# Third chunk of a retention recurrence in halves of 64 tokens, and one visit of the fourth chunk behind another inner product

## The chip, the cores and the metric

The kernel runs on one core of a Trainium2 chip. The metric is the device time of one execution in microseconds (us); the median of several executions is compared. Engines are named as in the profile: PE (TensorE matmul), PEld (its weight loads), DVE (VectorE), ACT (ScalarE), POOL (GpSimd), SP (SyncE, whose queue issues nearly all the DMAs).

## What is computed

A retention recurrence over 768 tokens (4 batches, 8 heads of 64 dimensions), whose output, with the heads side by side, goes through a feed-forward block of 512 by 2048 with a leaky ReLU:

```python
for t in range(S):
    state = gamma[None, :, None, None] * state + np.einsum('bhd,bhe->bhde', k[:, :, t], v[:, :, t])
    y[:, :, t] = scale * np.einsum('bhd,bhde->bhe', q[:, :, t], state)
x = y.transpose(0, 2, 1, 3).reshape(B * S, H * D)
h = x @ w_in
out = np.maximum(0.01 * h, h) @ w_out
```

Everything is in 32-bit floats.

## The kernel before

The tokens are worked in six chunks (c = 0 to 5) of 128 tokens per batch, 512 tokens in all. The feed-forward block of a chunk is worked in four units (u = 0 to 3) of 512 of the 2048 hidden columns. Both of its products use Strassen's seven products, named M1 to M7, each a group of eight matmul records on the full array.

Chunks 0 and 1 run first and together (`hidden` and `output`, recorded at L628). Each is a generator of seven steps; `run` calls, after each step, whatever the tables `hidden_more` and `output_more` (L1053 to L1075) list under s0 to s6 for (chunk, unit). In this phase the weights are unpacked too: `next_mantissas` on DVE (L556 to L568), whose ends let SP load the next pieces; the sums of the weights (`sum_of_unit`, L972) are formed, and `keep_unit` (L1001) stores each unit to DRAM.

Chunks 2 to 5 run in the loop at L1234, n = 0 to 15, four units for each chunk. The hidden product is there `inner(n, group)` (L1140) for two groups of output columns. It is written by hand: M1, M5, M4, M6, M2, M3, M7 into banks 0 to 3 of PSUM. ACT copies M1 from bank 0 to bank 3 (L1153), M6 is added to it there by PE, and the other results are copied out by ACT or added by DVE. `outer(n, 1)` (L1174) makes the four blocks of g from them: five sums on DVE and four leaky ReLUs on ACT (L1184). `output` with `room` puts M1 into bank 5, M5 into bank 7 and M6 into bank 4 (`room`, L1211: A, B, C, D are banks 5, 4, 7, 6), in the order M1, M5, M6, M2, M7, M3, M4. `products(steps, n)` lets n of these seven steps be issued. The units' weights stream back from DRAM into `wa` and `wb` (`load_unit`, L1024), for the next unit as soon as a group of the present one is done, or, where `held` is set, behind the visit that follows.

The recurrence of a chunk is a visit for two batches at a time, (c, 0) and (c, 2).

For c = 1 and 2 it has the old form: `score` (L149, matmuls at L165) for each batch, `masked` on DVE (L183, recorded at L185, 128x768), and for c = 2 `visit` (L331): `reads` of the old state (L200), `last_values` (L235), `state` (L250), `first_values` (L224), then `tokens_taken` (L280) and `state_taken` (L286) on DVE. Some of these matmuls use the array as four tiles of 64x64, others as two of 128x64.

For c = 3 to 5 it has the joined form, by halves of 64 tokens. `scores_of_pair` (L348) makes the scores within each half (L360) and the two halves' sums of k times v (L371), masks the scores on DVE (L378) and adds the sums to the old state one after the other (a state in the middle of the chunk, and one at its end). `joint_visit` (L399) then makes the outputs with `read` (L414) and `value` (L431) and takes them out with four operations on DVE (L453). All these matmuls are 64x64. Afterwards it loads k and v of the next pair into the same tiles (L307), has POOL decay v (`decay_v`, L135), and loads a later pair's q and k (`ahead`). PSUM of a joint visit: banks 1 and 7 for its first batch, 0 and 2 for its second; DVE takes the second batch first, and within a batch the second bank first.

What sets the order around the change: each engine issues its instructions in the order in which the program writes them; there is no planner. For chunk 2 the tables place it: scores of (2, 2) at s0 of `hidden` (1, 3), its visit at s4, scores of (2, 0) at s6, its visit at s2 of `output` (0, 3), followed at s3 by `differ(2)` (differences of x on DVE) and `next_heads` (loads of (3, 0) and (3, 1) and their decays on POOL); the sums of x for group 0 at s6. Then, at L1215 to L1232: three products of the last output of chunk 1, `scores_of_pair(3, 0)`, two products, `inner(0, 0)`, two products, `inner(0, 1)`, `outer(0, 1)`, and `joint_visit(3, 0)`. The loop then begins with the differences of g and `inner(1, 0)`. In the loop the visits (4, 0) and (5, 0) stand behind `inner(n + 1, 0)` of u = 0, and all (c, 2) behind that of u = 1; three products after each, `scores_of_pair` of the following pair is issued.

Of the kernel before, what the change touches and what calls it, by code (L numbers as in the profile page):

```python
# [9 lines left out]
FP32 = mybir.dt.float32  # L10
# [8 lines left out]
C = 128  # L19
# [3 lines left out]
def kernel(  # L23
# [82 lines left out]
    def place_for(c, b, place=None):  # L106

        if place is None:
            x = work.tile([128, 2, HP, C], FP32, tag="qk", bufs=AHEAD, name=f"qk_{c}_{b}")
            y = work.tile([128, 2, H, D], FP32, tag="kv", bufs=AHEAD, name=f"kv_{c}_{b}")  # L110
        else:
            flat = place.rearrange("p i k n -> p (i k n)")
            half = 2 * HP * C
            x = flat[:, 0:half].rearrange("p (s a t) -> p s a t", s=2, a=HP)
            y = flat[:, half : 2 * half].rearrange("p (s h d) -> p s h d", s=2, h=H)
        heads[c, b] = x, y
# [7 lines left out]
    def load_k(c, b):  # L124
        nc.sync.dma_start(out=heads[c, b][1][:, 0], in_=kv[c, b][:, 0])

    def load(c, b, place=None):
# [202 lines left out]

    def visit(c, b):  # L331

        for f in (reads, last_values, state, first_values):
            for i in range(2):
                f(c, b + i)
        for i in range(2):
            tokens_taken(c, b + i, xs[c][0])
        for i in range(2):
            state_taken(c, b + i, for_state(sums_at[c, b + i]))
        for i in range(2):  # L340
            heads.pop((c, b + i))

    halves_of_states = []
    state_of = [states[:, 2 * p : 2 * p + 2] for p in range(B // 2)]
    mid_of = {}
    quads = [(m, i, 2 * m + i) for m in range(HP // 2) for i in range(2)]

    def scores_of_pair(c, b):  # L348

        if b == 0:  # L350
            next_gq()
        at = [bank[j].rearrange("p (b m i t) -> p b m i t", b=2, m=HP // 2, i=2)
              for j in range(2)]
        sums = [bank[2 + h].rearrange("p (b a d) -> p b a d", b=2, a=HP) for h in range(2)]
        for n in range(2):
# [28 lines left out]
        old = state_of[p]  # L384
        mid = mid_of[p] = halves_of_states.pop(0)
        plus(mid, old, sums[0])
        state_of[p] = None
        if not last:
# [9 lines left out]

    def joint_visit(c, b):  # L399

        later = following(c, b)
        at = [[bank[k].rearrange("p (a t) -> p a t", t=C) for k in banks]
              for banks in ((1, 7), (0, 2))]
        by_half = mid_of.pop(b // 2)
# [43 lines left out]
        for n in (1, 0):  # L448
            for j in (1, 0):
# [4 lines left out]
                                        in1=gq[:, j], op=ALU.mult)  # L454
        if c < NC - 1:
            halves_of_states.extend(by_half)
        for n in range(2):
            heads.pop((c, b + n))
        if later is not None:
# [4 lines left out]
            for n in range(2):  # L464
                decay_v(later[0], later[1] + n)
        for n in range(2):
            ahead(c + 1, b + n)

    def following(c, b):
# [308 lines left out]

    def scored(c, b):
        def do():  # L780
            decay_v(c, b)
            score(c, b)
            masked(c, b)
        return do

    def differ(c):
# [259 lines left out]
    def next_heads():  # L1046
# [3 lines left out]
        for b in range(2):  # L1050
# [8 lines left out]
                     s4=[lambda: load(2, 2, place_of_unit(0, "in22"))],  # L1059
                     s5=[sum_of_unit(3, 0)], s6=[sum_of_unit(3, 1)]),  # L1060
        (1, 3): dict(s0=[begin_x(2), scored(2, 2), scored(2, 3)],
                     s1=[sum_of_unit(3, 2)], s2=[sum_of_unit(3, 3)],
                     s3=[keep_unit(3)], s4=[lambda: visit(2, 2)],
                     s6=[scored(2, 0), scored(2, 1)]),
    }
# [5 lines left out]
        (1, 2): dict(s0=[sum_of_unit(2, 3)], s1=[keep_unit(2)]),  # L1071
        (0, 3): dict(s0=[begin_units], s1=[lambda: differences(*parts[1][1:])],
                     s2=[lambda: visit(2, 0)], s3=[differ(2), next_heads],
                     s6=[sums(2, 0)]),
    }  # L1075
# [196 lines left out]

JOINED = 3

# [84 lines left out]
```

## Time and profile before

| what | us |
|---|---|
| median of 9 runs (lowest, highest) | 647.38 (645.43, 648.39) |
| the profiled execution's own time | 646.12 |
| its span, first to last instruction | 644.0 |
| PE busy | 633.8 |
| PEld busy | 570.3 |
| DVE busy | 461.3 |
| ACT busy | 269.7 |
| POOL busy | 22.2 |
| granted TensorE clock | 1.000 |

How to read it: the span is cut into stages by the program's order. Up to about 225 us the first two chunks and the weights' unpacking run, and chunk 2's recurrence lies at 191 to 220 us. The rest is the loop. A matmul in the source is two records in the trace. In the timeline a line gives the start of a run of records, its length up to the end of the last one, and, in brackets, how long the engine stood idle ahead of it and what released it. Matmul records overlap, so the time that a group takes is read from its start to the start of the next group.

### The profile page before, as it was taken

How to read it: one execution, taken by the hardware profiler on the slowest of the kernel's cores; microseconds unless marked ns; L12 is line 12 of the kernel's file. 1: busy time of each engine (PE TensorE's matmuls, PEld its weight loads, DVE VectorE, ACT ScalarE, POOL GpSimd, SP SyncE). 2: the span in 40 equal slices, each digit the busy share in tenths (PEclk: the TensorE clock that was granted, in tenths of full speed). 3: DMA queues.
4: the chain of work that ended last, by engine and by line, in shares of the span. 5: the costliest groups of instructions: out<-in, count | busy, mean ns of one | idle time of the engine just before them, and what ended most of it. 6: DMA issues, size and time to landing. Idle time of an engine off the chain costs nothing.

```text
span 644.0 us, 14045 instructions
## 1 busy us (share of the span) xinstructions
PE 633.8 (98%) x5958; PEld 570.3 (89%) x5958; DVE 461.3 (72%) x756; ACT 269.7 (42%) x515; POOL 22.2 (3%) x45
## 2 busy tenths in 40 slices
PE   8999999999999998999999999999999999999997
PEld 5888888888888897998999898999989999999996
DVE  5789769889979777466785756878737778636655
ACT  5875557257253033342342342523424423534421
POOL 2000000000011010101000101000010000000000
PEclk9999999999999999999999999999999999999999
DMA  8931327455965977637544584554456336444201
GB/s 330 404 122 60 104 66 256 136 195 152 309 241 177 330 255 242 238 89 246 160 127 161 181 257 158 174 172 152 144 185 194 89 117 195 156 157 159 87 0 67
DMA packets 89263, 113.40 MB, mean 176 GB/s; under 512 B 3432, under 2 KB 71912, under 8 KB 89200
## 3 DMA queue, kind: packets, MB, share of 16 engines
q1 hardware_dynamic: 88896, 111.88, 52.6%
q8 instruction: 47, 0.77, 0.5%
q10 hardware_dynamic: 304, 0.62, 0.3%
q14 instruction: 16, 0.13, 0.1%
HBM read 93.35 MB, written 19.14 MB: 175 GB/s over the span
## 4 chain that ended last, share of the span: by engine, by line
PE 91%; DMA 4%; DVE 2%; ACT 1%; SPq 0%; issue 0%; DVEq 0%
PE bank L628 31%; PE bank L1149 27%; PE C_h L628 4%; PE B_o L628 4%; PE A_o L628 4%; PE A_h L628 4%; PE B_h L628 4%; PE C_o L628 4%; PE D_o L628 2%; PE D_h L628 2%; DMA kv<-in_kv_dram 2%; DMA x_words<-in_weights_dram 1%; DMA in<-in_kv_dram 1%; PE bank L360 1%; PE bank L371 1%; PE ap L165 1%
## 5 line engine op out<-in xcount | busy, mean ns | idle before, releaser
L572 DVE TENSOR_TENSOR made<-made,bank 128x512 f32<-128x512 f32 (+1 forms) x96 | 56.4, 618 | 61.1 <-PE bank L1149 56.8
L572 DVE TENSOR_TENSOR o<-o,bank 128x512 f32<-128x512 f32 (+2 forms) x91 | 58.5, 660 | 53.2 <-PE bank L628 31.8
L628 PE MATMUL bank<-g,w 128*128 128x256 f32 x384 | 89.8, 382 | 0.0
L1149 PEld LDWEIGHTS bank<-x,wb 128*128 128x128 f32 x672 | 77.6, 192 | 1.4 <-issue 0.5
L628 PEld LDWEIGHTS bank<-g,w 128*128 128x128 f32 x384 | 70.7, 190 | 9.1
L1149 PE MATMUL bank<-x,wb 128*128 128x128 f32 x672 | 77.9, 275 | 0.3 <-issue 0.3
L1149 PE MATMUL bank<-x,wa 128*128 128x128 f32 x512 | 68.8, 276 | 3.1 <-DVE x L453 3.1
L1149 PEld LDWEIGHTS bank<-x,wa 128*128 128x128 f32 x512 | 63.8, 192 | 4.8 <-DVE x L453 3.2
L628 PE MATMUL bank<-gd,w 128*128 128x256 f32 x288 | 66.6, 381 | 0.1
L628 PEld LDWEIGHTS bank<-gd,w 128*128 128x128 f32 x288 | 54.3, 190 | 9.1 <-DVE x L453 1.9
L1184 ACT ACTIVATE g<-g 128x512 f32<-128x512 f32 x64 | 39.5, 631 | 34.2 <-DVE g L572 34.2
L1149 PE MATMUL bank<-t,wa 128*128 128x128 f32 x384 | 53.3, 275 | 0.0
L1149 PEld LDWEIGHTS bank<-t,wa 128*128 128x128 f32 x384 | 48.0, 192 | 0.0
L1153 ACT COPY bank<-bank 128x512 f32<-128x512 f32 (+1 forms) x32 | 16.7, 522 | 68.4 <-PE bank L1149 66.8
L572 DVE TENSOR_TENSOR g<-made 128x512 f32<-128x512 f32 x64 | 42.7, 688 | 1.2
L721 ACT COPY bank<-bank 128x512 f32<-128x512 f32 x17 | 9.7, 570 | 71.1 <-PE bank L628 71.0
L575 DVE TENSOR_TENSOR gd<-g,gd 128x512 f32<-128x512 f32 x48 | 33.2, 692 | 4.9
L739 ACT COPY bank<-bank 128x512 f32<-128x512 f32 x16 | 9.1, 570 | 46.2 <-PE bank L628 46.2
L628 PE MATMUL bank<-g,last 128*128 128x256 f32 x120 | 28.1, 380 | 0.0
L628 PE MATMUL bank<-gd,last 128*128 128x256 f32 (+1 forms) x124 | 27.5, 373 | 0.0
L628 PE MATMUL A_h<-x,w 128*128 128x256 f32 x112 | 26.6, 380 | 0.0
L628 PEld LDWEIGHTS bank<-gd,last 128*128 128x128 f32 x124 | 22.9, 190 | 3.3 <-DVE gd L575 0.3
(195 smaller groups left out, 1027.8 us busy)
## 6 DMA issues: line engine op xcount, KB each, us to landing
wa<-kept SPq DMA_DIRECT2D x16, 1344.0 KB, 8.0
raw<-in_weights_dram SPq DMA_DIRECT2D x31, 512.0 KB, 4.3
wb<-kept SPq DMA_DIRECT2D x16, 896.0 KB, 5.3
kv<-in_kv_dram SPq DMA_DIRECT2D x28, 256.0 KB, 5.2
wa<-kept SPq DMA_DIRECT2D x16, 448.0 KB, 4.2
wb<-kept SPq DMA_DIRECT2D x16, 448.0 KB, 6.1
out_dram<-o SPq DMA_DIRECT2D x23, 256.0 KB, 4.0
kept<-w SPq DMA_DIRECT2D x12, 448.0 KB, 5.9
```

Of the source, the lines that this page charges most:

```text
L165: nc.tensor.matmul(to, lhsT=x[ts(j, 64), 1, a, ts(late, 64)], rhs=x[ts(j, 64), 0, a, late * 64 :], start=True, stop=True, skip_group_check ...
L360: nc.tensor.matmul(at[j][ts(h, 64), n, m, i], lhsT=x[ts(j, 64), 1, a, ts(h, 64)], rhs=x[ts(j, 64), 0, a, ts(h, 64)], start=(n == 0 and a = ...
L371: nc.tensor.matmul(sums[h][ts(j, 64), n, a], lhsT=y[ts(h, 64), 0, 2 * a + j], rhs=y[ts(h, 64), 1, 2 * a + j], start=(n == 0 and a == 0), s ...
L572: nc.vector.tensor_tensor(out=out, in0=a, in1=b, op=ALU.add)
L575: nc.vector.tensor_tensor(out=out, in0=a, in1=b, op=ALU.subtract)
L628: nc.tensor.matmul(to, lhsT=block(w, sa)[:, k, ts(i, 128)], rhs=rhs[:, k, a:z], start=(first and (i == 0 or split) and n == 0 and k == 0), ...
L721: nc.scalar.copy(out=bank_of("B"), in_=ps)
L739: nc.scalar.copy(out=bank_of("D"), in_=ps)
L1149: nc.tensor.matmul(ps[q][:, i], lhsT=w[:, j, i], rhs=part_of(moving[i], s), start=(i == 0 and m in ("M1", "M5", "M4")), stop=True, skip_gr ...
L1153: nc.scalar.copy(out=ps[3], in_=ps[0])
L1184: nc.scalar.activation(g[:, i], g[:, i], AF.Prelu, alpha=0.01)
```

## The change

Chunk 2 gets the joined form too: `JOINED` goes from 3 to 2, `score`, `masked` and `visit` are replaced by `early_scores` and `early_visit`, which call `scores_of_pair` and `joint_visit` with PSUM tiles of the first phase's pool (two tiles of two banks, in turn). The state in the middle of the chunk gets room behind the loaded q, k and v of a pair of batches (`rooms`, `spare`), and one more tile of states is added. The decays of (2, 2) and (2, 3) are issued one step earlier, those of (2, 0) and (2, 1) as before; the scores of (2, 0) go from s6 of `hidden` (1, 3) to s0 of `output` (0, 3), and its visit from s2 to s3 there.

`scores_of_pair(3, 0)` is issued after four products of chunk 1's last output, where it was three. `joint_visit(3, 0)` goes from ahead of the loop into it, behind `inner(1, 0)` and `outer(1, 0)`, and the load of the next unit's `wa` behind it.

The PSUM of every joint visit in the loop changes: banks 1 and 2 for the first batch, 0 and 7 for the second, so that bank 7 is the first that DVE takes out, where it was the third.

```diff
+            if place.shape[1] == 7:
+                rooms[b] = flat[:, 2 * half : 2 * half + 2 * HP * D]
...
-    def visit(c, b):
-
-        for f in (reads, last_values, state, first_values):
-            for i in range(2):
-                f(c, b + i)
-        for i in range(2):
-            tokens_taken(c, b + i, xs[c][0])
-        for i in range(2):
-            state_taken(c, b + i, for_state(sums_at[c, b + i]))
...
-    halves_of_states = []
+    halves_of_states = [const.tile([128, 2, HP, D], FP32, name="more_states")]
+    free_again = {}
...
-    def joint_visit(c, b):
-
-        later = following(c, b)
-        at = [[bank[k].rearrange("p (a t) -> p a t", t=C) for k in banks]
-              for banks in ((1, 7), (0, 2))]
+    def joint_visit(c, b, banks=None):
+
+        later = following(c, b) if c > JOINED else None
+        banks = banks or [[bank[k] for k in at] for at in ((1, 2), (0, 7))]
+        at = [[ps.rearrange("p (a t) -> p a t", t=C) for ps in of_one] for of_one in banks]
...
+    def early_scores(c, b, place):
+        def do():
+            banks = [pair_of_banks(f"{name}_{c}_{b}") for name in ("ap", "sp")]
+            scores_of_pair(c, b, banks[0] + banks[1], place())
+        return do
+
+    def early_visit(c, b):
+        def do():
+            joint_visit(c, b, [pair_of_banks(f"yp{n}_{c}_{b}") for n in range(2)])
+        return do
...
-                     s5=[sum_of_unit(3, 0)], s6=[sum_of_unit(3, 1)]),
-        (1, 3): dict(s0=[begin_x(2), scored(2, 2), scored(2, 3)],
+                     s5=[sum_of_unit(3, 0)], s6=[sum_of_unit(3, 1), early_decays(2, 2)]),
+        (1, 3): dict(s0=[begin_x(2), early_scores(2, 2, spare(3))],
                      s1=[sum_of_unit(3, 2)], s2=[sum_of_unit(3, 3)],
-                     s3=[keep_unit(3)], s4=[lambda: visit(2, 2)],
-                     s6=[scored(2, 0), scored(2, 1)]),
+                     s3=[keep_unit(3)], s4=[early_visit(2, 2)],
+                     s6=[early_decays(2, 0)]),
...
-        (0, 3): dict(s0=[begin_units], s1=[lambda: differences(*parts[1][1:])],
-                     s2=[lambda: visit(2, 0)], s3=[differ(2), next_heads],
+        (0, 3): dict(s0=[begin_units, early_scores(2, 0, spare(2))],
+                     s1=[lambda: differences(*parts[1][1:])],
+                     s3=[early_visit(2, 0), differ(2), next_heads],
                      s6=[sums(2, 0)]),
...
-    products(last, 3)
-    halves_of_states.extend(work.tile([128, 2, HP, D], FP32, tag=tag, name=f"half_{tag}")
-                            for tag in ("u2", "m5"))
+    products(last, 4)
+    halves_of_states.append(work.tile([128, 2, HP, D], FP32, tag="m5", name="half_states"))
     scores_of_pair(3, 0)
     for b in range(2):
         ahead(3, 2 + b)
-    products(last, 2)
+    products(last, 1)
     sums_of_x(2, 1)
     inner(0, 0)
     outer(0, 0)
     products(last, 2)
     inner(0, 1)
     outer(0, 1)
-    xs[3] = new_x(3)
-    joint_visit(3, 0)
...
-        visiting = c + 1 < NC and (u == 1 or u == 0 and n > 0)
+        visiting = c + 1 < NC and u < 2
...
-JOINED = 3
+JOINED = 2
```

The layout of the inputs in DRAM and a small table of decays follow `JOINED`; they are made ahead of the launch or in one matmul of the same kind as before.

More of the change, by code (lines that the diff above doesn't have):

```diff
@@ L125, in load_k, with spare @@
         nc.sync.dma_start(out=heads[c, b][1][:, 0], in_=kv[c, b][:, 0])
+    rooms = {}
+    def spare(b):
+        return lambda: rooms[b].rearrange("p (n a d) -> p n a d", n=2, a=HP)
     def load(c, b, place=None):
@@ L329 @@
     weights_of = {}
-    def visit(c, b):
-        for f in (reads, last_values, state, first_values):
-            for i in range(2):
-                f(c, b + i)
-        for i in range(2):
-            tokens_taken(c, b + i, xs[c][0])
-        for i in range(2):
-            state_taken(c, b + i, for_state(sums_at[c, b + i]))
-        for i in range(2):
-            heads.pop((c, b + i))
-    halves_of_states = []
+    halves_of_states = [const.tile([128, 2, HP, D], FP32, name="more_states")]
+    free_again = {}
     state_of = [states[:, 2 * p : 2 * p + 2] for p in range(B // 2)]
@@ L346, with scores_of_pair @@
     quads = [(m, i, 2 * m + i) for m in range(HP // 2) for i in range(2)]
-    def scores_of_pair(c, b):
-        if b == 0:
+    def scores_of_pair(c, b, banks=None, mid=None):
+        if b == 0 and c > JOINED:
             next_gq()
-        at = [bank[j].rearrange("p (b m i t) -> p b m i t", b=2, m=HP // 2, i=2)
+        banks = banks or bank
+        at = [banks[j].rearrange("p (b m i t) -> p b m i t", b=2, m=HP // 2, i=2)
               for j in range(2)]
-        sums = [bank[2 + h].rearrange("p (b a d) -> p b a d", b=2, a=HP) for h in range(2)]
+        sums = [banks[2 + h].rearrange("p (b a d) -> p b a d", b=2, a=HP) for h in range(2)]
         for n in range(2):
@@ L384, in scores_of_pair @@
         old = state_of[p]
-        mid = mid_of[p] = halves_of_states.pop(0)
+        free_again[p] = [old]
+        if mid is None:
+            mid = halves_of_states.pop(0)
+            free_again[p].append(mid)
         plus(mid, old, sums[0])
-        state_of[p] = None
         if not last:
@@ L454, in joint_visit @@
                                         in1=gq[:, j], op=ALU.mult)
-        if c < NC - 1:
-            halves_of_states.extend(by_half)
+        halves_of_states.extend(free_again.pop(b // 2))
         for n in range(2):
@@ L465, in joint_visit, with pair_of_banks, early_decays, do @@
                 decay_v(later[0], later[1] + n)
-        for n in range(2):
+        for n in range(2) if c > JOINED else ():
             ahead(c + 1, b + n)
+    def pair_of_banks(name):
+        ps = two_banks(name).rearrange("p j a t -> p j (a t)")
+        return [ps[:, j] for j in range(2)]
+    def early_scores(c, b, place):
[7 more added lines that the diff above has]
+        return do
+    def early_decays(c, b):
+        def do():
+            for n in range(2):
+                decay_v(c, b + n)
+        return do
     def following(c, b):
@@ L777, in run @@
                 do()
[L779 to L784, printed above, removed]
     def differ(c):
```

## The prediction

> **What bounds the kernel now.** I read the page's busy shares first, then its costliest groups, then PE's timeline around the edits.
>
> ```profile
> PE 633.8 (98%) x5958; PEld 570.3 (89%) x5958; DVE 461.3 (72%) x756; ACT 269.7 (42%) x515; POOL 22.2 (3%) x45
> ...
> L1149 PE MATMUL bank<-x,wa 128*128 128x128 f32 x512 | 68.8, 276 | 3.1 <-DVE x L453 3.1
> ...
> L628 PEld LDWEIGHTS bank<-gd,w 128*128 128x128 f32 x288 | 54.3, 190 | 9.1 <-DVE x L453 1.9
> ```
>
> PE is the bound: what leaves PE's queue is gained, unless a wait takes its place. The second line shows one stall of 3.1 us, the third 1.9 us of late weight loads; both wait for DVE's taking out of a visit (L453). A group of eight L628 records takes 1.73 us, start to start, wherever nothing interrupts. In these timelines a block's price is the time between its neighbours' starts, less 1.73 for each whole group of eight.
>
> ```profile
> 205.58 1.89 PE L628 MATMUL B_h<-x,w 128*128 128x256 f32 x8
> 207.56 1.57 PE L165 MATMUL ap<-qk 64*64 64x128 f32 x64
> 209.06 1.99 PE L628 MATMUL A_o<-g,last 128*128 128x256 f32 x8
> 210.89 1.89 PE L628 MATMUL C_o<-gd,last 128*128 128x256 f32 x8
> 212.62 1.89 PE L628 MATMUL B_o<-gd,last 128*128 128x256 f32 x8
> ...
> 218.11 1.99 PE L628 MATMUL D_o<-gd,last 128*128 128x256 f32 x8
> 219.94 1.89 PE L628 MATMUL A_o<-g,last 128*128 128x256 f32 x8
> ```
>
> The old form's scores of (2, 0) cost 210.89 - 205.58 - 2 x 1.73 = 1.85; its visit 219.94 - 212.62 - 2 x 1.73 = 3.86.
>
> ```profile
> 227.28 3.62 PE L628 MATMUL bank<-gd,last 128*128 128x256 f32 x16
> 230.83 1.16 PE L360 MATMUL bank<-qk 64*64 64x64 f32 x64
> 231.81 1.14 PE L371 MATMUL bank<-kv 64*64 64x64 f32 x64
> 232.87 3.72 PE L628 MATMUL bank<-g,last 128*128 128x256 f32 x16
> ...
> 246.14 4.85 PE L1149 MATMUL bank<-x,wb 128*128 128x128 f32 x42
> ...
> 256.09 0.49 PE L1149 MATMUL bank<-x,wa 128*128 128x128 f32 x2 [3.08 <-DVE x L453]
> ...
> 288.06 0.46 PE L431 MATMUL bank<-am,kv 64*64 64x64 f32 x16
> ...
> 290.09 1.99 PE L628 MATMUL bank<-g,w 128*128 128x256 f32 x8
> 292.03 3.72 PE L628 MATMUL bank<-gd,w 128*128 128x256 f32 x16
> ```
>
> The joined form's scores and sums cost 2.22 (228 to 233 us: 236.43 - 227.28 - 4 x 1.73 = 2.23). Its visit costs 2.22: 287.97, where inner's last record leaves, to 290.09, and 0.10 that the first full-array group takes longer. The first group behind it then runs 1.94, where 1.83 is usual behind small matmuls.
>
> **Part 1: chunk 2 in the joined form.** Before: 1.70 (scores of (2, 2), 191.47 to 192.97 and its neighbours), 3.86, 1.85, 3.86, together 11.27. After: 4 x 2.22 = 8.88. PE gains **2.39**. The joined form issues 512 records where there were 384; a record costs it 1.09 us / 64 = 17 ns (L360). [...]
>
> DVE does not follow for nothing. Masking and states of (2, 2) took 1.74 us as two L185 (194.85 to 196.59) with the states later; now two masks and two state sums stand there together, 2.60 (232.04 to 234.64 in the same form). So the weight unpacking behind them runs 0.86 later; DVE has no gap from 196.6 to 207.7. The tokens of (2, 2), taken from 205.85, start at 206.71 and end four operations later (1.41) at 208.12. PE, ahead by then, wants those banks for scores (2, 0) at 207.92 (191.38 + 2.22 + 4 x 1.73 + 2.22 + 3 x 1.73): a wait of **0.25**.
>
> The same 0.86 delays SP. Its load of k and v for (2, 1) at 201.60 waited for L561 on DVE, and the stores and loads queued behind it fill the DMA engines from 204 to 232 us (share 0.93 to 1.11 in each stretch of 4 us). At their end are the loads of chunk 3's first pair:
>
> ```profile
> 228.29 1.33 POOL L135 TENSOR_TENSOR kv<-kv,dec 128x512 f32<-128x512 f32 x1 [12.50 <-DMA kv<-in_kv_dram]
> 230.90 1.04 POOL L135 TENSOR_TENSOR kv<-kv,dec 128x512 f32<-128x512 f32 x1 [1.28 <-PE bank L628]
> ```
>
> The second decay ended at 231.94 and L371's second half needed it at 232.35: slack 0.4. (The release named on the second line was long done; v, issued at 222.78, landed 8.0 us later, at 230.8.) The visit itself ends at 217.8, as before (218.1), so it does not hold these loads; SP reaches them at 217.54 + 0.86. The decay then ends at 232.80. PE, 2.14 ahead but with one product more in front, wants it at 231.9: a wait of **0.9**, on the path, with all of PE behind it. Bounds: 0.1, if the DMA engines absorb the delay, and 1.9, if the landing takes 1 us more. I take 0.9, from the row.
>
> `inner(0, 0)` then follows one product sooner behind the scores. DVE finishes its state sums at about the scores' end + 1.6, `inner`'s first copy into bank 3 comes at + 2.7: no cost. The x sums of group 0 end near 228.3, 7 us ahead of their use. The moved fifth store and q, k loads on SP have more than 20 us.
>
> **Part 2: `joint_visit(3, 0)` behind `inner(1, 0)`.** Before, from the end of `inner(0, 1)` (246.14 + 4.69 = 250.83) to the output's first group (262.45): 11.62 = visit 2.2, stall 3.1, inner 6.25. The stall's reason goes: `inner(1, 0)` no longer waits for the tokens in banks 0 and 2. But what is late next? ACT:
>
> ```profile
> 249.69 0.48 ACT L1161 COPY made<-bank 128x384 f32<-128x384 f32 x1
> 252.88 1.23 ACT L1184 ACTIVATE g<-g 128x512 f32<-128x512 f32 x2 [2.71 <-DVE g L572]
> 254.80 1.23 ACT L1184 ACTIVATE g<-g 128x512 f32<-128x512 f32 x2 [0.70 <-DVE g L572]
> ```
>
> The four leaky ReLUs of `outer(0, 1)` wait for DVE's five sums and end at 256.03. In ACT's order the copy of M1 of `inner(1, 0)` into bank 3 is next; M6 needs it, and PE works in order. M1, M5, M4 run from 250.83 to 253.51, then PE stands until 256.03 + 0.57 + 0.05 = 256.65: a stall of 3.1, the same size. M6 to M7 take 3.57, the visit 2.22: 262.44, against 262.45. I take **0.0**; bounds -3.1 (no stall) and +0.5 (DVE's or ACT's chain a little later). The next `wa`, 242.88 + 7.1 = 250.0 before, is wanted 5 us sooner, at 251.1, with another 3.1 under the stall.
>
> Behind the moved visit its four k and v loads have less time: L371 comes 6.4 us after it, as behind (4, 0), where the decays ended at 370.39 and L371 began at 371.38; but one load behind (4, 2) came 0.24 too late for PE (400.21). **+0.15**, bounds 0 and 0.4.
>
> **Part 3: bank 7 taken out first.** Behind each joint visit, M5 of the output writes bank 7, third of four to be taken out:
>
> ```profile
> 290.89 1.41 DVE L453 TENSOR_TENSOR x<-bank,dec 128x256 f32<-128x256 f32 x4
> ```
>
> The third ends at 290.89 + 0.67 + 0.41 = 291.97 and M5 starts at 292.03. First, it is free at 291.30, 0.5 ahead of need. Each wait cost 0.11 and 0.10 in the restart; at 364.61 it was 0.41 in all. Five visits: 4 x 0.21 + 0.41 = 1.25. Behind (4, 2) PE then waits for the late load instead (0.21 lost), and at (4, 0) I grant 0.3 of 0.41. I take **-0.93**; bounds -1.25 and 0.
>
> **Sum.** -2.39 + 0.25 + 0.9 + 0.0 + 0.15 - 0.93 = -2.0. Against the profiled execution (span 644.0, own time 646.12) that is 644.1; it lies 1.26 below the median of 647.38, and the median is what is compared: **645.4**.
>
> **Rivals.**
> - *The load is not late:* DMA absorbs the 0.86, wait 0.1. Then -2.8, or -3.85 with every bound of part 3 and no token wait: about 644.5 to 643.5. For: a lull near 216 us (5 to 9 tenths of the engines). Against: it stems from a chain of waits that shifts too.
> - *The stall really goes,* M1's copy not held by the leaky ReLUs: -5.1, 642.3. Against: ACT's program order has the four activations ahead of the copy. [...]
> - *Nothing to see:* the load costs 1.9, part 3 yields 0.3, part 2 costs 0.5: -2.39 + 0.25 + 1.9 + 0.5 + 0.15 - 0.3 = +0.1, 647.5.
> - *Slower:* the second unit's `wa` (L1032). `inner(1, 0)` asks for it 5 us sooner; one for one it delays PE once it lands after 251.1 + 3.1 = 254.2. To turn -2.0 into +1.3 it must land at 257.5, 14.6 us after issue; the longest `wa` landing in busy stretches was 10.2. 649 or more.
>
> **Chances.** Forecast 0.50, load not late 0.18, stall gone 0.07, nothing to see 0.17, slower 0.08. The range takes in the first rival's low end and most of the third: 643.5 to 647.1. A measurement of this kernel tells about 0.2% (1.3 us) from no change. Faster: 0.45 of the forecast's 0.50, plus 0.18 and 0.07: 0.70. Same: 0.05 + 0.17 = 0.22. Slower: 0.08.
>
> **What would show it.** Chunk 2's four blocks at 2.2 each; a PE wait of about 0.9 in L371 ahead of the loop, released by POOL; PE idle about 3.1 us inside `inner(1, 0)`, released by ACT's L1153 copy, no longer by L453; the 1.9 us of PEld waiting for L453 gone. Wrong, if L371 waits not at all or over 2 us, or if that stall is under 1 us.

## The result, and the profile after

| kernel | median us (lowest, highest) | executions | ratio to before, 95% interval |
|---|---|---|---|
| before | 647.96 (645.43, 651.41) | 55 | |
| changed | 645.22 (643.68, 649.45) | 18 | 0.9969 [0.9955, 0.9982] |

The change makes the kernel faster by 2 us (the forecast's sum was -2.0). The ratio goes with the means of the executions, 645.92 against 647.93; the medians differ by 2.7. The forecast time was 645.4. The profiled execution of the changed kernel has a span of 642.6 and an own time of 644.33, at a granted clock of 0.999. Line numbers move: before's L628, L1149, L1153, L1184, L360, L371, L431, L453 and L135 are now L648, L1163, L1167, L1198, L357, L368, L430, L452 and L142.

First the page of the changed kernel, busy shares and costliest groups (the last column is the idle time ahead of the group and what ended it):

```profile
PE 631.2 (98%) x6086; PEld 569.6 (89%) x6086; DVE 461.0 (72%) x760; ACT 269.5 (42%) x515; POOL 22.2 (3%) x45
...
L1163 PE MATMUL bank<-x,wa 128*128 128x128 f32 x512 | 68.9, 276 | 2.9 <-ACT bank L1167 2.9
...
L648 PEld LDWEIGHTS bank<-gd,w 128*128 128x128 f32 x288 | 54.7, 190 | 7.4
```

PE has 128 records more and is busy 2.6 us less. The stall of L1163 is still there, 2.9 where it was 3.1, but ACT now ends it. The 1.9 us of weight loads that waited for the taking out of a visit are gone.

Chunk 2 in PE's timeline of the changed kernel (start, length, engine, line, records):

```profile
207.51 1.89 PE L648 MATMUL A_o<-g,last 128*128 128x256 f32 x8
209.34 1.16 PE L357 MATMUL ap<-qk 64*64 64x64 f32 x64
210.32 1.13 PE L368 MATMUL sp<-kv 64*64 64x64 f32 x64
...
213.21 1.89 PE L648 MATMUL B_o<-gd,last 128*128 128x256 f32 x8
214.93 1.89 PE L648 MATMUL D_o<-gd,last 128*128 128x256 f32 x8
216.75 0.46 PE L430 MATMUL yp<-am,kv 64*64 64x64 f32 x16
...
220.61 1.89 PE L648 MATMUL C_o<-g,last_s 128*128 128x256 f32 x8
```

By the prediction's way of counting, scores and sums of (2, 0) cost 213.21 - 207.51 - 2 x 1.73 = 2.24, and the visit 220.61 - 214.93 - 2 x 1.73 = 2.22. There is no wait in front of the scores at 209.34.

Ahead of the loop, the scores and sums of (3, 0), on PE and then on POOL:

```profile
231.50 0.69 PE L357 MATMUL bank<-qk 64*64 64x64 f32 x32
232.64 0.69 PE L357 MATMUL bank<-qk 64*64 64x64 f32 x32 [0.45 <-DMA qk<-in_qk_dram]
233.16 0.65 PE L368 MATMUL bank<-kv 64*64 64x64 f32 x32
234.48 0.69 PE L368 MATMUL bank<-kv 64*64 64x64 f32 x32 [0.68 <-POOL kv L142]
```

```profile
230.63 1.04 POOL L142 TENSOR_TENSOR kv<-kv,dec 128x512 f32<-128x512 f32 x1 [12.46 <-DMA kv<-in_kv_dram]
233.38 1.04 POOL L142 TENSOR_TENSOR kv<-kv,dec 128x512 f32<-128x512 f32 x1 [1.71 <-PE bank L357]
```

PE waits here for the second batch twice: for its q and k, which the forecast had left out, and then for the decay of its v, which ends at 234.42, 0.06 ahead of its use.

The second unit's first inner product, on PE and then on ACT:

```profile
252.22 1.95 PE L1163 MATMUL bank<-x,wa 128*128 128x128 f32 x16
257.08 1.38 PE L1163 MATMUL bank<-x,wa 128*128 128x128 f32 x10 [2.90 <-ACT bank L1167]
```

```profile
253.38 1.23 ACT L1198 ACTIVATE g<-g 128x512 f32<-128x512 f32 x2 [2.71 <-DVE g L592]
255.31 1.23 ACT L1198 ACTIVATE g<-g 128x512 f32<-128x512 f32 x2 [0.70 <-DVE g L592]
256.44 0.58 ACT L1167 COPY bank<-bank 128x512 f32<-128x512 f32 x1
```

ACT runs four leaky ReLUs of the first unit, and only then the copy of M1 that M6 needs. PE stands from 254.2 to 257.08.

Behind the visit (3, 2), on PE:

```profile
290.62 1.99 PE L648 MATMUL bank<-g,w 128*128 128x256 f32 x8
292.45 1.89 PE L648 MATMUL bank<-gd,w 128*128 128x256 f32 x8
...
295.99 1.16 PE L357 MATMUL bank<-qk 64*64 64x64 f32 x64
```

The first full-array group takes 1.83, where it took 1.94: M5 no longer waits for bank 7. From M1 to the scores it is 295.99 - 290.62 = 5.37, where it was 295.68 - 290.09 = 5.59.

Three stages, from the starts in PE's timelines, show where the time went in each kernel that was run. "First" goes from the last `A_h` group ahead of chunk 2's first scores (it starts at 185.67 in the changed kernel, 184.47 before) to `inner(0, 0)`; "second" from there to the visit (3, 2); "third" from there to the end of the last matmul.

| kernel | first | second | third | clock | median us | n | ratio to before |
|---|---|---|---|---|---|---|---|
| before | 51.96 | 51.63 | 351.88 | 1.000 | 647.96 | 55 | |
| changed | 51.27 | 51.65 | 350.53 | 0.999 | 645.22 | 18 | 0.9969 [0.9955, 0.9982] |
| e1_banks_back | 50.03 | 53.50 | 351.68 | 0.997 | 646.85 | 12 | 0.9983 [0.9965, 1.0001] |
| e2_visit_ahead | 49.71 | 54.52 | 351.67 | 0.995 | 646.51 | 12 | 0.9978 [0.9960, 0.9997] |
| e3_wb_later | 49.71 | 53.30 | 351.67 | 0.997 | 645.11 | 5 | 0.9949 [0.9931, 0.9967] |
| e4_m1_first | 54.81 | 51.12 | 352.68 | 0.997 | 642.98 | 12 | 0.9934 [0.9912, 0.9956] |
| e5_kept_busy | 51.79 | 52.27 | 351.26 | 1.000 | 646.08 | 12 | 0.9980 [0.9957, 1.0003] |
| e6_chunk2_alone | 53.16 | 53.26 | 352.14 | 0.997 | 648.93 | 12 | 1.0010 [0.9994, 1.0026] |
| e7_chunk2_old | 52.01 | 54.74 | 350.81 | 0.997 | 647.03 | 12 | 0.9973 [0.9958, 0.9989] |
| e8_both | 49.72 | 50.77 | 350.69 | 1.000 | 641.41 | 6 | 0.9899 [0.9875, 0.9923] |
| e9_changed_again | 49.71 | 52.27 | 351.17 | 1.000 | 645.40 | 12 | 0.9967 [0.9944, 0.9990] |
| e10_wb_later_again | 49.70 | 54.32 | 350.36 | 0.997 | 644.73 | 11 | 0.9950 [0.9930, 0.9971] |
| e11_wb_later_kept_busy | 49.71 | 52.59 | 352.72 | 1.000 | 645.58 | 12 | 0.9955 [0.9936, 0.9974] |
| e12_chunk2_wb_later | 49.70 | 53.15 | 351.71 | 0.997 | 644.44 | 8 | 0.9946 [0.9927, 0.9965] |

The stages and the clock are those of one profiled execution each; medians and ratios are of all executions. e1 to e4, e5 to e8 and e9 to e12 are three sets on three chips, each with executions of the kernel before beside it, to which its ratios refer.

### The profile page after: what moved, and what is told of

Same layout as the page of the kernel before. It is cut to its first block, busy times and chain, and to the rows that moved or that the text cites. A ratio compares the mean times of both kernels' runs of the same rounds, so it can differ in the third digit from the quotient of the medians.

```text
span 642.6 us, 14314 instructions
## 1 busy us (share of the span) xinstructions
PE 631.2 (98%) x6086; PEld 569.6 (89%) x6086; DVE 461.0 (72%) x760; ACT 269.5 (42%) x515; POOL 22.2 (3%) x45
## 4 chain that ended last, share of the span: by engine, by line
PE 93%; DMA 3%; DVE 1%; ACT 1%; SPq 1%; issue 0%; POOL 0%; DVEq 0%
PE bank L648 30%; PE bank L1163 27%; PE C_h L648 4%; PE A_h L648 4%; PE C_o L648 4%; PE A_o L648 4%; PE B_h L648 4%; PE B_o L648 4%; DMA qk<-in_qk_dram 2%; PE D_o L648 2%; PE D_h L648 2%; PE d L669 2%; PE bank L430 1%; DMA kv<-in_kv_dram 1%; PE bank L413 1%; PE bank L368 1%
## 5 line engine op out<-in xcount | busy, mean ns | idle before, releaser
L648 PE MATMUL bank<-g,w 128*128 128x256 f32 x384 | 89.9, 382 | 0.0
L648 PEld LDWEIGHTS bank<-g,w 128*128 128x128 f32 x384 | 70.7, 190 | 9.2
L1163 PEld LDWEIGHTS bank<-x,wb 128*128 128x128 f32 x672 | 77.6, 192 | 0.8
L1163 PE MATMUL bank<-x,wb 128*128 128x128 f32 x672 | 77.6, 275 | 0.0
L1163 PE MATMUL bank<-x,wa 128*128 128x128 f32 x512 | 68.9, 276 | 2.9 <-ACT bank L1167 2.9
L1163 PEld LDWEIGHTS bank<-x,wa 128*128 128x128 f32 x512 | 63.8, 192 | 4.7 <-ACT bank L1167 3.9
L648 PE MATMUL bank<-gd,w 128*128 128x256 f32 x288 | 66.1, 379 | 0.0
L648 PEld LDWEIGHTS bank<-gd,w 128*128 128x128 f32 x288 | 54.7, 190 | 7.4
L1198 ACT ACTIVATE g<-g 128x512 f32<-128x512 f32 x64 | 39.5, 631 | 34.2 <-DVE g L592 34.2
L1163 PE MATMUL bank<-t,wa 128*128 128x128 f32 x384 | 53.3, 275 | 0.0
L1163 PEld LDWEIGHTS bank<-t,wa 128*128 128x128 f32 x384 | 48.0, 192 | 0.0
L1167 ACT COPY bank<-bank 128x512 f32<-128x512 f32 (+1 forms) x32 | 16.7, 522 | 67.0 <-PE bank L1163 66.7
L648 PE MATMUL bank<-g,last 128*128 128x256 f32 x120 | 28.3, 380 | 0.0
L648 PE MATMUL bank<-gd,last 128*128 128x256 f32 (+1 forms) x124 | 27.5, 373 | 0.0
L648 PE MATMUL A_h<-x,w 128*128 128x256 f32 x112 | 26.6, 380 | 0.0
L648 PEld LDWEIGHTS bank<-gd,last 128*128 128x128 f32 x124 | 22.9, 190 | 3.3 <-DVE gd L595 0.3
```

The lines of the kernel that those rows point to most:

```text
L648: nc.tensor.matmul(to, lhsT=block(w, sa)[:, k, ts(i, 128)], rhs=rhs[:, k, a:z], start=(first and (i == 0 or split) and n == 0 and k == 0), ...
L1163: nc.tensor.matmul(ps[q][:, i], lhsT=w[:, j, i], rhs=part_of(moving[i], s), start=(i == 0 and m in ("M1", "M5", "M4")), stop=True, skip_gr ...
L1167: nc.scalar.copy(out=ps[3], in_=ps[0])
L1198: nc.scalar.activation(g[:, i], g[:, i], AF.Prelu, alpha=0.01)
```

## The experiments

Theory: chunk 2 gives 2.24 on PE and the late loads of (3, 0) and (3, 1) take part of it back; the moved visit gives nothing, because ACT's queue takes DVE's place as the end of the stall; the order of the banks gives about 1.2. Rivals: the moved visit or the banks bring all of it, or the loads do not matter.

### One part undone

e1_banks_back: banks 1 and 7 for the first batch again.

```diff
-        banks = banks or [[bank[k] for k in at] for at in ((1, 2), (0, 7))]
+        banks = banks or [[bank[k] for k in at] for at in ((1, 7), (0, 2))]
```

> The changed kernel with the PSUM banks of the joint visits as before (1 and 7, 0 and 2); all else as changed. Theory (bank 7 taken out first is worth about 1.3 us in PE's time behind the visits): each output behind a visit shows PEld waiting for the tokens again, M1 to the scores takes 5.6 us where the changed kernel shows 5.4, over six visits 1.2 to 1.5 us in all, part of which may vanish behind loads that land late; time 0.8 to 1.5 us above the changed kernel, ratio to the kernel before 0.998 to 0.9995. Rival (the wait was free, because the scores behind it wait for loads of k and v anyway): within 0.3 us of the changed kernel, ratio about 0.997.

The ratio is 0.9983, 0.0014 (0.9 us) above the changed kernel's, with intervals that overlap. In the profile the waits of weight loads for L452 are back (over six visits), and from the visit (5, 2) to the end there are 147.07 again, where the changed kernel has 146.85: 0.2 for that visit.

```profile
L648 PEld LDWEIGHTS bank<-gd,w 128*128 128x128 f32 x288 | 54.2, 190 | 9.0 <-DVE x L452 1.9
```

From M1 to the scores it is 5.59 again behind four visits and 5.41 behind (4, 0). In every profile with bank 7 first it is 5.37 to 5.38 behind all of them, and in the others (before, e1, e6, e12) 5.59, and 5.40 to 5.79 behind (4, 0). So 0.2 for each visit is shown in PE's rows; the time alone would not prove it.

e2_visit_ahead: the visit (3, 0) ahead of the loop again.

```diff
     inner(0, 1)
     outer(0, 1)
+    xs[3] = new_x(3)
+    joint_visit(3, 0)
...
-        visiting = c + 1 < NC and u < 2
+        visiting = c + 1 < NC and (u == 1 or u == 0 and n > 0)
```

> The changed kernel with the first visit of the fourth chunk ahead of the loop again, in front of the second unit's first inner product; all else as changed. Theory (the stall only changes its cause): PE idles about 3.1 us for the tokens (L452) ahead of that inner product and no longer for ACT inside it; from the end of the inner product before to the output's first group 11.5 to 11.7 us as in both kernels; time within 0.4 us of the changed kernel. Rival (the move is what gained): 2 to 3 us above the changed kernel, ratio to the kernel before about 1.000 or more.

The ratio is 0.9978, 0.6 us above the changed kernel's, again within the intervals. The stall is 3.08, released by L452 on DVE; in the changed kernel it is 2.90, by ACT. The second stages compare best between profiled executions in which the clock was lowered behind this stall: with the visit moved 53.50, 53.30, 54.32, 54.74 (e1, e3, e10, e7), with the visit ahead 54.52, 53.26, 53.15 (e2, e6, e12). In e2 PE is slowed for longer: from the end of the stall to the output's first group it takes 9.24 us, against 7.98 in e6, 7.87 in e12 and 6.36 in before, whose clock stays at 1.00 there. e10 and e7 have a wait that the visit ahead never has, for the k and v that are loaded behind the moved visit. In e10:

```profile
269.79 0.69 PE L368 MATMUL bank<-kv 64*64 64x64 f32 x32 [0.80 <-DMA kv<-in_kv_dram]
```

It is 1.32 in e7, 0.95 in e4, 0.60, 0.38 and 0.28 in e8, e9 and e5, and absent in four of the ten profiles with the visit moved and in all four with the visit ahead. The move gains nothing that shows, and costs up to this wait.

e7_chunk2_old: the kernel before with the new banks and the moved visit. Chunk 2 keeps its old form, and the scores of (3, 0) stay behind three products.

```diff
-              for banks in ((1, 7), (0, 2))]
+              for banks in ((1, 2), (0, 7))]
...
-    xs[3] = new_x(3)
-    joint_visit(3, 0)
...
-        visiting = c + 1 < NC and (u == 1 or u == 0 and n > 0)
+        visiting = c + 1 < NC and u < 2
```

> The kernel before with chunk 2 left in its old form, and the other parts of the change: the visit (3, 0) behind the inner product, the new banks, bank 7 first. By the forecast's terms: 0.0 + 0.15 - 0.93 = -0.8, ratio 0.9988; by the profile after: -0.08 - 1.28 + 0.4 = -0.95, ratio 0.9985. The stall of 2.9 is there, released by ACT's copy, no PE wait for the loads of (3, 1). Together with the kernel with chunk 2 alone it should give the whole, 0.9969; a sum far from it says that the parts act on one another. Rival (the moved visit is worth the stall): -3 or more, ratio 0.995.

The ratio is 0.9973 [0.9958, 0.9989], 1.75 us faster than before, where 0.8 to 0.95 was expected; the interval holds both. The first stage is 52.01, as before; the third 350.81, near the changed kernel's. The stall is 2.91, ended by ACT.

### One part alone

e6_chunk2_alone: the kernel before with chunk 2's joined form and nothing else of the change.

```diff
+        banks = banks or [[bank[k] for k in at] for at in ((1, 7), (0, 2))]
...
-        (0, 3): dict(s0=[begin_units], s1=[lambda: differences(*parts[1][1:])],
-                     s2=[lambda: visit(2, 0)], s3=[differ(2), next_heads],
+        (0, 3): dict(s0=[begin_units, early_scores(2, 0, spare(2))],
+                     s1=[lambda: differences(*parts[1][1:])],
+                     s3=[early_visit(2, 0), differ(2), next_heads],
...
-JOINED = 3
+JOINED = 2
```

> The kernel before with chunk 2's joined form alone: banks 1 and 7 first as before, the scores of (3, 0) behind three products, the visit (3, 0) ahead of the loop. By the forecast's own terms: -2.39 on PE, +0.25 and +0.9 for the two late arrivals, so -1.2, ratio 0.998. By the profile after: -2.24, no wait for tokens, and at the scores of (3, 0) between 0 and 1.5, with three products in front of them rather towards 1.5 to 2.5, so 0 to -2.2, ratio 0.9966 to 1.000. The stall inside the second inner product stays at 3.1, released by L453's counterpart on DVE, and the 1.9 of late weight loads stay. Rival (chunk 2's form brings nothing, the gain is all from the banks and the visit): ratio 1.000 with the four blocks at 2.8 each.

It brings nothing: 1.0010 [0.9994, 1.0026]. The forecast's own terms (0.998) fall; the end at which the loads take everything holds. The profile says why. PE's timeline at the scores and sums of (3, 0), which here stand behind three products:

```profile
229.35 0.69 PE L357 MATMUL bank<-qk 64*64 64x64 f32 x32 [0.39 <-DMA qk<-in_qk_dram]
231.92 0.69 PE L357 MATMUL bank<-qk 64*64 64x64 f32 x32 [1.88 <-DMA qk<-in_qk_dram]
...
233.75 0.69 PE L368 MATMUL bank<-kv 64*64 64x64 f32 x32 [0.67 <-POOL kv L142]
```

Three waits, 2.94 us in all. PE reached these scores about 2.2 sooner, the loads did not, and the gain was waited away. The rival (no gain in the form) fails too, for the four blocks in it still cost 2.2 to 2.4 each. The fourth product in front of these scores, which looked like a detail of the change, gives the loads 1.73 more; e2, which has it and the new banks besides, is at 0.9978. It was not run alone. Together e6 and e7 make 0.9983, where the whole has 0.9969; the intervals are too wide to tell whether the parts act on one another.

### The late loads

e3_wb_later: the first load of wb, issued ahead of the loads of (3, 0) and (3, 1), goes behind them.

```diff
     def begin_units():
...
-        load_unit(0, 1)
...
-                     s3=[early_visit(2, 0), differ(2), next_heads],
+                     s3=[early_visit(2, 0), differ(2), next_heads, lambda: load_unit(0, 1)],
```

> The changed kernel with the first load of wb (1.3 MB, wanted only at 246 us) issued behind the loads of the fourth chunk's first pair instead of ahead of them. Theory (the 1.1 us that PE idles in that pair's scores and sums are these loads landing late behind a full DMA queue): the loads are issued about 2 us sooner and land 3 us sooner or more, PE's idle there goes from 1.13 us to 0, the scores and sums take 2.2 to 2.3 us where they take 3.8, time 1.2 to 1.6 us below the changed kernel, ratio to the kernel before 0.9945 to 0.995. Rival (POOL's decays or the bandwidth are late whatever the order): the idle stays above 0.7 us and the time within 0.4 us of the changed kernel.

The ratio is 0.9949, from five executions, and there is no wait at the scores of (3, 0). But e1 and e2 had next to none either without this edit (0.33 and 0.01 above 49.70 in the first stage), so it was run again, beside the changed kernel.

> The changed kernel as it is, beside the three others on one chip, as their base. From its 19 executions so far: median about 645.2, ratio 0.9969, most executions with a mean clock of 0.997 or lower (16 of 19 so far). If late loads and lowered clocks differ from chip to chip, ratio and clocks here tell how far: up to 1 us to either side.

> The changed kernel with only wb's first load moved behind the loads of (3, 0) and (3, 1), again, as the base of the next run. Theory (the late loads cost 1.1 to 1.7 in an execution, and lowered the clock in some): 0.5 to 1.5 below the changed kernel of this call, no wait at the scores of (3, 0), a mean clock of 0.997 in most executions from the stall of 2.9 inside the inner product, and hardly any below. Rival (the load's lateness doesn't depend on wb's place): same time and same clocks as the changed kernel of this call.

The changed kernel repeats: 0.9967. With wb later the ratio is 0.9950; the medians differ by 0.7 us, in the lower half of what was expected, but the intervals overlap, and the clocks are no better (0.999 or 1.0 in 2 of 11 executions, against 3 of 12), so the two medians alone decide nothing. In the profiled execution of the changed kernel the late load is absent this time (first stage 49.71), in e10 too. All profiles together say more: in the seven profiles of chunk 2's joined form with wb first, the first stage is above 49.70 by 1.57, 0.33, 0.01, 5.11 (a group slowed by 1.0 in it), 2.09, 3.46 and 0.01; in the five with wb later by 0.00 to 0.02. The wait differs from execution to execution, and with wb later no profile has it.

e12_chunk2_wb_later: e6 with the same edit.

> The kernel with chunk 2's joined form alone, and wb's first load behind the k and v loads of (3, 0) and (3, 1). Chunk 2 alone gave 1.001. Theory (its 2.24 of PE time are there and the late loads of (3, 0) and (3, 1) gave them back): with the loads ahead of wb the waits of 0.39, 1.88 and 0.67 at the scores of (3, 0) shrink to under 0.7 together, the clock is lowered once (behind the stall) as in the kernel before, and the median is 1.5 to 2.3 below before, ratio 0.9965 to 0.9977. Rival (the time is lost elsewhere, in the moved decays or the states): ratio 0.999 to 1.002 again.

The ratio goes from 1.0010 to 0.9946 [0.9927, 0.9965], intervals apart, and no wait is left at these scores:

```profile
228.56 1.16 PE L357 MATMUL bank<-qk 64*64 64x64 f32 x64
```

That is 3.5 us faster than before, more than the 2.24 on PE. Of the rest, 0.36 lies outside the span: own time less span is 2.09 in before (median of 29 executions, 2.03 to 2.21) and in e7 2.10, but 1.70 to 1.75 in each kernel with chunk 2 joined. About 0.9 is not accounted for, within the interval. e12 has neither the moved visit, nor the new banks, nor the fourth product, and is no slower than e10, which has all three (0.9946 against 0.9950). Once the loads are in time, the medians show no gain from the rest of the change, though e7 showed 1.75 for the visit and the banks alone; the runs leave this open.

### The stall inside the inner product

e4_m1_first: M1 of `inner(1, 0)`, with its copy, ahead of `outer(0, 1)` and its leaky ReLUs.

```diff
-    def inner(n, group, held=False):
+    def inner(n, group, held=False, which=range(7)):
...
-        for m, q, j, s in INNER:
+        for m, q, j, s in (INNER[i] for i in which):
...
-        if not held:
+        if not held and 6 in which:
...
     inner(0, 1)
+    inner(1, 0, which=range(1))
     outer(0, 1)
...
-            inner(n + 1, 0, held=visiting)
+            inner(n + 1, 0, held=visiting, which=range(n == 0, 7))
```

> The changed kernel with M1 of the second unit's first inner product, and ACT's copy of it into bank 3, issued ahead of the four leaky ReLUs of the unit before; all else as changed. Theory (PE's 2.9 us idle inside that inner product is M6 waiting for this copy, which stands behind the four activations in ACT's order): the copy starts as soon as DVE has freed bank 3, near 252.6 us instead of 256.4, M6 no longer waits, and what is late next is M3, which needs M5's copy, still behind the activations: idle 1.2 to 1.6 us there, gain 1.3 to 1.7 us on the changed kernel, ratio to the kernel before 0.9943 to 0.995. Rival (the inner product waits for something else, the load of wa or the sums on DVE): idle stays near 2.9 us, same time as the changed kernel.

The median is 642.98, ratio 0.9934 [0.9912, 0.9956], an interval that just touches the changed kernel's: 2.2 us below it, a little more than the 1.9 by which the stall got shorter. The mean clock is 0.999 or 1.0 in 7 of 12 executions, and in 6 of 31 of the changed kernel, so the lowered clock may be the rest. In its timeline the stall is under 1 us, and what is late next is a later copy:

```profile
259.64 0.49 PE L1163 MATMUL bank<-x,wa 128*128 128x128 f32 x2 [0.98 <-ACT made L1169]
```

So the four leaky ReLUs in front of M1's copy were the cause. The profiled execution itself is a bad one (own time 648.5): 2.49 us of waiting for q and k at 233.71, 0.73 for a decay at 235.60, and behind that a full-array group of 2.84 (236.66 to 239.50), where 1.83 is usual.

e8_both puts e3's and e4's edits together.

> The changed kernel with both edits that helped alone: wb's first load issued behind the k and v loads of (3, 0) and (3, 1), and M1 of the second unit's first inner product with its copy ahead of the four leaky ReLUs. Theory: no late load at the scores of (3, 0) beyond 0.5 us, and no gap over 1 us inside the second inner product, hence no lowered clock in either place; most executions at a mean clock of 1.0, median 641.5 to 642.5, ratio 0.990 to 0.992, and a narrower spread than with M1 first alone (641.2 to 648.5). Rival (the late load varies with the DMA engines' traffic and not with wb's place in the queue): no better than M1 first alone, 643.0, ratio 0.9934, with the same spread.

The median is 641.41, ratio 0.9899 [0.9875, 0.9923], with no wait at the scores of (3, 0), a stall of 1.11, and 1.0 as the mean clock of five of six executions. Both theories hold in it, and it is faster than the kernel before and the changed one, with intervals apart. It differs from e10 by e4's edit alone and is 3.3 us below it, again with intervals apart; the stall is 1.8 shorter, and e10 has 1.0 in 2 of 11 executions.

### What a gap does to the clock

e5_kept_busy fills the stall with matmuls whose results nobody reads.

```diff
             elif m == "M4":
                 nc.scalar.copy(out=sums[:, 2], in_=ps[2])
+                for i in range(idle):
+                    nc.tensor.matmul(bank[5][:, ts(i % 4, C)], lhsT=w[:, j, i % 4],
+                                     rhs=part_of(moving[i % 4], s), start=True, stop=True,
+                                     skip_group_check=True)
...
-            inner(n + 1, 0, held=visiting)
+            inner(n + 1, 0, held=visiting, idle=12 * (n == 0))
```

> The changed kernel with 12 further matmuls (24 records of 112 ns, 2.7 us) between M4 and M6 of the second unit's first inner product. Their results go to a bank that nobody reads, so they are work that is thrown away; they fill the stall of 2.9 us that waits for ACT's copy of M1, and PE has no long gap there. Theory (a gap of about 3 us lowers the granted clock behind it, at about 2 us a time): the clock stays at 1.0 between 250 and 262 us, the records of L1163 behind M4 take 56 ns each and not double, executions with a mean clock of 0.997 become rare and those of 0.994 become 0.997, and the median falls from 645.2 by 1 to 2 us, to about 643.2 to 644.2, though PE has 2.7 us more to do. Rival (the drop has another cause, such as the work before it): the granted clock has the same spread as before, and the median stays at 645.2 or rises by up to 0.3, what of the 2.7 us sticks out of the stall.

e11_wb_later_kept_busy is the same edit on e10's kernel.

> The run before with the 12 further matmuls that fill the stall inside the second unit's first inner product; what they compute is thrown away. With the late loads gone, only that stall is left as a cause of a lowered clock. Theory (a lowered clock behind a gap costs 1.5 to 2.1 where it comes): nearly all executions at 1.0, and a median 1.0 to 2.0 below that of the run before. Rival (the clock's drop costs nothing that the end feels, or further work brings as much elsewhere): the clock at 1.0 and the same median within 0.5.

Half of the theory holds. The records of L1163 behind the filled stall take 112 ns each (in e5 six from 257.87 to 258.54), the undisturbed rate (before: 42 from 246.14 to 250.83); the 56 that was expected is in no row. The clock stays up: a mean of 0.999 or 1.0 in 15 of these 24 executions, against 20 of 103 in the changed kernel and its variants that keep a stall of 2.9 or more, and 23 of 88 in before. No fall of the time shows: 646.08 and 645.58, against 645.40 for the changed kernel and 644.73 for e10. The rival's time holds (0.9955 against 0.9950 for e10). In the profiles e11's second stage is 1.73 below e10's and its third 2.36 above; where the gain went shows only in part, in PE's timeline of e11:

```profile
299.70 1.67 PE L648 MATMUL bank<-g,w 128*128 128x256 f32 x7 [2.30 <-issue]
```

PE waits 2.30 here and 0.78 at 273.35 for nothing that the profile shows. The last section comes back to it.

## Why the prediction was right, step by step

**Part 1, PE: right.** Forecast -2.39, measured -2.25: the first stage is 51.96 before, and 49.70 in every profile in which no load is late. The blocks of the joined form cost 2.21, 2.36, 2.24 and 2.22. That is 17.6 ns for a 64x64 record (9.03 us for 512), near the working's 17. The working's 1.09 us for 64 records is in no row: L360's took 0.98 from start to start and L371's 1.06, which is 15 and 17 ns.

**Part 1, the wait for tokens: 0.25 forecast, none found.** DVE's last taking out ended at 209.06, and PE wanted the bank at 209.24. The working had DVE 0.2 behind PE; it was 0.2 ahead.

**Part 1, the late load: right in kind, too small, and not a constant.** Forecast 0.9 with bounds 0.1 to 1.9, at the decay of (3, 1). The profile of the changed kernel has 0.45 of idle time for q and k and 0.68 for the decay, together 1.57 of the stage from start to start; other profiles of it or its near kin have 0.01 (e9, e2), 0.33 (e1) and 2.09 (e5). The working followed v alone; q and k of the same batch stand in the same queue, and they came too late as well. Both the forecast and the rival "the load is not late" are thus true, in different executions: by the prediction's own sign (no wait in L371) it would have been wrong in e9's, which is the same kernel. The low end of that rival, -3.85, does not come out of its terms, -2.39 + 0.1 - 1.25 = -3.54.

**Part 2, the moved visit: right.** Forecast 0.0, since ACT's four leaky ReLUs end the stall in DVE's place; measured 2.90 by L1167 against 3.08 by L453, and a second stage of 51.65 against 51.63. e4 shows the cause by removing it. The rival "the stall really goes" had 642.3; with the cause removed, e4 has 642.98. The rival "slower", by a late wa, did not occur: in no profile does PE wait for wa here. The +0.15 for k and v behind the moved visit, with a bound of 0.4, was too small for most executions: that wait was absent in the changed kernel's first profile, but 0.28 to 1.32 in six of the ten with the visit moved.

**Part 3, the banks: right.** Raw forecast 1.25: the time from M1 to the scores behind the five visits (behind the last, to the next inner product) falls from 5.59, 5.79, 5.59, 5.59 and 7.22 to 5.37, 5.37, 5.38, 5.37 and 7.01, 1.28 in all. The 5.79 is particular to that execution (5.40 to 5.41 in e1, e6 and e12); without it there is 0.9. Net forecast -0.93; the third stage gives -1.35 in the changed kernel's first profile and -0.71 in e9's. The two differ between the visits (4, 2) and (5, 0), 73.53 against 74.14, where e9 has a wait of 0.40 for k and v.

**The sum.** The three stages of the two profiled executions give -0.69, +0.02 and -1.35, together -2.02, the forecast's sum. That it fits so closely is luck: the terms had -1.24 for the first stage, +0.15 for the second and -0.93 for the third, and the errors (+0.55, -0.13, -0.42) cancel; e9's stages give -2.25, +0.64 and -0.71, together -2.32. Three parts outside the stages were not forecast: +1.20 ahead of them (a start that differs between executions: 0.68 of issue wait at 24.32, for one), -0.6 from the last matmul to the end of the span, and -0.4 outside the span, so that the own times differ by -1.79 in all. What makes the last two is open.

**The base.** The prediction set its sum from an execution 1.26 below the median without a reason for that distance. The reason is the clock: that execution's mean is 1.000, and before's executions at 1.0 have medians of 646.1 to 646.4, as the last section tells. It holds for both kernels (the changed kernel's profiled execution lies 0.89 below its median, at 0.999), so the difference stood.

## What to carry to other kernels

When the bounding engine gets work sooner, look up every load that it will meet sooner, all of a batch and not only the one that was last before; here 2.24 us on PE, taken alone, was worth nothing (e6) until the loads had been moved ahead of one that nobody needed yet (e12). Before a wait is taken away, read the program order of the engine that comes next: the stall kept its size under another name, and one copy issued ahead of four activations (2.2 us, e4) was worth more than the whole move (nothing that shows, e2). In seven of the ten profiles with a gap of 2.9 to 3.1 us on TensorE, it cost 1.5 to 2.9 us more than its length, so medians must be set beside the granted clock.

## What the runs showed of the hardware

**A gap of 2.9 to 3.1 us can halve the granted clock behind it.** The windows of e10 behind the stall of 2.91 that ends at 254.56 (columns: window, length, busy time and records of PE, PEld, DVE, ACT and POOL, granted clock, DMA share, GB/s):

```profile
254.00:256.00 2.00, 1.44 (x8) 1.44 (x9) 1.83 (x3) 1.50 (x4) 0.00 (x0) 0.76 0.45 120
256.00:258.00 2.00, 2.00 (x12) 2.00 (x11) 0.15 (x1) 0.61 (x2) 0.00 (x0) 0.50 0.00 0
258.00:260.00 2.00, 2.00 (x20) 1.88 (x19) 0.69 (x1) 0.56 (x1) 0.00 (x0) 0.89 0.00 0
```

At 0.50, PE issues 12 records in 2 us, and 20 in the next 2 at 0.89. An estimate from these rows, with the clock at 1.00 otherwise, is 0.96 + 2 + 0.44 = 3.4 us at 0.50. From the end of the stall to the visit this execution takes 259.96 - 254.56 = 5.40, the changed kernel's first profile, at 1.00 throughout, 260.84 - 257.08 = 3.76: 1.64 lost (1.53 in e7). Before's executions show the same by their mean clock: medians of 646.1, 646.2 and 646.4 at 1.0 in the three sets, 648.3, 647.7 and 648.0 at 0.997. Of the ten profiles with a stall of 2.9 or more, seven show PE slowed there: 5.29 to 5.40 to the visit in e1, e3, e7 and e10, and 7.87 to 9.24 to the output's first group in e2, e6 and e12, where before takes 6.36. The same stall left the clock at 1.00 in those of before, changed and e9, so the drop depends on the execution. Gaps of 2.91 to 3.08 were enough for it; in e4 2.49 with 0.73 more 1.2 us later were (2.84 for the group behind them), and e6's 0.39, 1.88 and 0.67 at the scores of (3, 0) were not (3.56 for the two groups behind them, as in before). What else decides it was not shown.

**Near 300 us PE waits for nothing that the profile shows, and longer where the stall was filled or shortened.** Many profiles have there a wait put down to "issue". In the ten with a stall of 2.9 or more in front of or inside `inner(1, 0)` it is 0 to 0.52, and the six with none have 0.39 to 0.74 there for a load or for ACT; in the four in which that stall is 0.23 to 1.11 (e4, e5, e8, e11) it is 1.75, 1.34, 0.68 and 2.30, with 0.78 more in e11. The DMA queues of e11 and its window under that wait:

```profile
q8 instruction: 48, 0.79, 0.5%
```

```profile
297.00:299.70 2.70, 0.40 (x1) 0.22 (x2) 1.68 (x3) 0.00 (x0) 0.00 (x0) 1.00 1.09 357
```

The page names a DMA queue "instruction", with 48 packets for 0.79 MB over the whole execution (47 for 0.77 in before), and the engines are full while PE waits, at a share of 1.09. They are as full in e10 at that place (1.02 from 297 to 299.7, 1.08 from there to 303), where the wait is 0.52. What PE waits for, and whether that queue has a part in it, was not shown; the two waits of e11 come to 2.30 + 0.78 = 3.08 us. That a filled gap is given back in this way is read from 14 profiles, one for each run, and wasn't tested by an experiment. Against a simple account stands e4, which came to this place 4 us later than before (306.09 against 302.27) and still waited 1.75.
